# Attention and expert FFN on one core: routing sums earlier, transposes in twos, expert tiles turned elsewhere

## The chip, the cores and the metric

The kernel runs on one core of a Trainium2 chip. The metric is the device time of one execution in microseconds (us). Three timed runs of the kernel before gave 311.85, 312.05 and 313.8 us, with a median of 312.05 us. Engines are named as in the profile: PE (TensorE matmul), PEld (its weight loads), DVE (VectorE), ACT (ScalarE), POOL (GpSimd) and SP (SyncE, which here only issues transfers).

## The reference

Eight sequences of 576 tokens, with 8 heads of 64, go through attention that is causal by blocks of 64. Each token's 512 values then go through the one expert that a hash of its id names: two matmuls with a ReLU between them.

```python
scores = scale * np.matmul(q, k.transpose(0, 1, 3, 2))          # q, k, v: (8, 8, 576, 64)
scores = np.where(block_i >= block_j, scores, -1e9)             # blocks of 64 positions
attn = softmax(scores);  x = np.matmul(attn, v) -> (4608, 512)
expert_idx = token_ids * 2654435761 % 8
for e in range(8):                                              # w1: 512x1024, w2: 1024x512
    out[mask_e] = np.maximum(x[mask_e] @ w1[e], 0.0) @ w2[e]
```

## The kernel before

The order on every engine is that in which the code is written; nothing is scheduled afterwards. A tile's buffers are shared out by pools, and an instruction that needs a buffer waits until its last reader is done.

**Attention.** A sequence's 8 heads are worked on as 4 pairs, so the loop at L590 runs over 32 pairs g and two more rounds that only finish. Pair g belongs to sequence b = g // 4, and r = g % 4 is its place there. In a round PE computes the scores of pair g in three chunks (`S_chunk`, L222, written here S0, S1, S2), ACT takes the exponentials of each (L234, "exp"), and PE multiplies the probabilities of pair g - 2 with v in two halves (`PV`, L260). `norm` (L278) on DVE divides the result and thereby frees the PSUM tile `O`, of which there is one. So the first half of `PV` in a round waits for the `norm` of the round before. Score tiles `ps` have two buffers, so a chunk waits for the exp two chunks back. In the first round of a sequence `S_rest` adds one small chunk.

**Transposes of q and k.** The next sequence c needs q and k transposed. That is done in six groups of 12 transposes (`T_sixth`, L194; PE at L179), each followed by one copy out of PSUM (L186, on DVE; for sequence 1 every second one on ACT). The PSUM tile `tp` has two buffers. The list `at` (L580 to L584) says in which round and at which of five places each group stands: 0 ahead of S0, 1 behind S0, 2 behind S1, 3 behind S2, 4 behind `norm`.

**Routing.** `route` (L331) is a generator on DVE with a few matmuls. Each `next(rgen)` runs it to its next yield. For each sequence it makes one-hot tiles (`one_hots`, L322 to L326) and adds up slots by five matmuls (L430, into a `tp` buffer, added up at L433 or L435). `STEPS` and `TABLE` say in which rounds it goes on. The last steps (rounds 21 to 23) write the tables by which rows are gathered.

**From attention to FFN.** `write_x` (SP, L297) stores a sequence's result in `x_dram`. `load_x` (POOL, L306) gathers 128 rows of one expert. The first three tiles of each expert hold rows of sequences 0 to 5 alone, so they wait for the write of sequence 5; the last two wait for that of sequence 7. `turn_x` (L494) transposes one gathered tile (4 transposes, then one DVE copy, L499). `stage_a_early` (L501) computes two of the eight output blocks of expert 0's first matmul while attention ends. `stage_a` (L657) and `stage_b` (L675) are the two matmuls of the FFN; `stage_b` can take a list of tiles to turn, one behind each of its groups of eight matmuls.

Of the kernel before, what the change touches and what calls it, by code (L numbers as in the profile page):

```python
# [24 lines left out]
EB, ES = 6, 384  # L25
G = CAP // 128
# [12 lines left out]
def kernel(  # L39
# [248 lines left out]
    GE = ES // P  # L288
# [26 lines left out]
    def digits(out, tmp, src, shift, mask):  # L315
        nc.vector.tensor_single_scalar(tmp[:, 0, :, :], src[:], mask, op=ALU.bitwise_and)
        nc.vector.tensor_single_scalar(tmp[:, 1, :, :], src[:], shift, op=ALU.arith_shift_right)
        nc.vector.tensor_copy(out[:], tmp[:])
# [167 lines left out]
    NPAIRS = B * NP  # L486
# [69 lines left out]
    rgen = route()  # L556
# [14 lines left out]
    tok2 = rt.tile([P, 2, B, 5], I32, name="tok2", tag="i2")  # L571
    tokb = rt.tile([P, 2, B, 5], BF16, name="tokb")
    digits(tokb, tok2, toki, 6, 63)


    turned = {}
    for c in range(1, B):
        f = NP * c
        if c == 1:
            at = ((2, 4), (3, 1), (3, 2), (3, 3), (3, 4), (3, 4))  # L580
        elif c < 6:
            at = ((f - 3, 2), (f - 3, 3), (f - 2, 2), (f - 2, 3), (f - 1, 0), (f - 1, 3))
        else:
            at = ((f - 4, 3), (f - 3, 2), (f - 3, 3), (f - 2, 3), (f - 1, 0), (f - 1, 3))  # L584
        for n, gp in enumerate(at):
            turned.setdefault(gp, []).append((c, n))

    STEPS = {0: 3, 1: 2, 2: 1, 8: 1, 12: 1, 21: 1, 22: 1, 23: 1}
    TABLE = (8, 12, 16, 20)
    for g in range(NPAIRS + 2):  # L590
        b, r = divmod(g, NP)

        def turn(at):
            for c, n in turned.get((g, at), ()):
                T_sixth(c, n)
# [7 lines left out]
        if g < NPAIRS:  # L603
            S_chunk(g, 1)
        turn(2)
        if g == 3:
            next(rgen)
        if g < 2:
            fill(3)
        if g >= 2:  # L610
# [1 line left out]
        if g < NPAIRS:  # L612
            S_chunk(g, 2)
            if r == 0:
                S_rest(b)
        if g in TABLE or g == 3:
            next(rgen)
        turn(3)

        if g == NPAIRS - 1:  # L620
            for tt in range(GE):
                turn_x(0, tt, psT)
        if g >= NPAIRS:
            stage_a_early(0, g - NPAIRS)
        if g >= 2:
            PV(g - 2, 1)
            norm(g - 2)
        turn(4)
        for _ in range(STEPS.get(g, 0)):
            next(rgen, None)  # L630
        if r == 0 and b + 2 < B:
# [7 lines left out]
        if g == 23:  # L639
            after(load_w1(0), vparts[B - 1][1], "these bytes are wanted first")  # L640
            load_w1(1)
        if NPAIRS - 4 <= g < NPAIRS - 4 + GE:
            load_x(0, g - NPAIRS + 4, g - NPAIRS + 5)
        if g == NPAIRS:
            load_x(1, 0, GE)
            load_w2(0)
# [7 lines left out]
    psH = ffn_ctx.enter_context(tc.tile_pool(name="psH", bufs=2, space=PSUM))  # L654
    psX = ffn_ctx.enter_context(tc.tile_pool(name="psX", bufs=2, space=PSUM))
    psY = ffn_ctx.enter_context(tc.tile_pool(name="psY", bufs=2, space=PSUM))
    def stage_a(e, c0, c1, f0=0):  # L657
        w1b, _ = wtiles[e]
        xT, hT = xTs[e], hTs[e]
        parts = [(c0, c1)] if c1 - c0 <= 512 else [(c0, c0 + HC), (c0 + HC, c1)]  # L660
        n = parts[0][1] - parts[0][0]
        for ft in range(f0, NFT):
            hp = psH.tile([P, 2, 512], F32, name="hp", tag="hp")
            for db in range(NKT):
                for t, (p0, p1) in enumerate(parts):
                    nc.tensor.matmul(  # L666
                        hp[:, t, 0:n], lhsT=w1b[:, db, ft * P : (ft + 1) * P], rhs=xT[:, db, p0:p1],
                        start=(db == 0), stop=(db == NKT - 1),
                    )
            nc.scalar.activation(hT[:, ft, c0:c1].rearrange("p (t n) -> p t n", n=n),  # L670
                                 hp[:, 0 : len(parts), 0:n], ACT.Relu)

    out_writes = []

# [48 lines left out]
    for e in range(3):  # L723
        load_x(e, GE, G)
    load_w2(1)
    stage_a(0, 0, ES, 2)
    for tt in range(GE):
        turn_x(1, tt, psX)
    stage_a(1, 0, ES)
    stage_b(0, 0, GE)  # L730
    for tt in range(GE, G):
        turn_x(0, tt, psX)
    for e in range(E):
        if e + 2 < E:
            load_w1(e + 2)
# [204 lines left out]
```

## Time and profile before

| | |
|---|---|
| median of three timed runs | 312.05 us |
| the profiled execution | 310.51 us |
| its span, first to last instruction | 308.7 us |
| PE busy | 262.9 us (85%) |
| ACT busy | 149.6 us (48%) |
| DVE busy | 138.5 us (45%) |
| POOL busy | 133.1 us (43%) |

Attention runs from about 12 to 145 us of the span, with the switch to the FFN at about 134 to 145 us, and the FFN from there to about 300 us. The rows further down come from three views. The timeline has one line for a run of like instructions: its start in the span, how long it took, the engine, the source line, what is written from what, and in square brackets how long the engine had been idle and what released it. The table of windows gives each engine's busy time in a stretch. The view of a source line gives its instructions and how long its transfers took to land.

### The profile page before, as it was taken

To read this page: it belongs to the slowest core of one execution; us is meant where nothing else is said; L and a number is where in the kernel's file an instruction comes from. 1 tells how busy PE (TensorE), PEld (TensorE's weight loads), DVE (VectorE), ACT (ScalarE), POOL (GpSimd) and SP (SyncE) were. 2 spreads that over 40 slices of the span, in tenths; PEclk is the share of its full clock that TensorE was granted. 3 is DMA by queue.
4 is the path that set the end of the run, shared out by engine and by line. 5 is a ranking of instruction groups with operands and counts; after the bars stand their busy time and mean duration, and the time that the engine had idled before them with its cause. 6 is when DMAs were issued, how large, how long until landed. Compare 5 with 4: busy or idle time off the path is not lost. (4 is left out here: it accounts for less than half of the span.)

```text
span 308.7 us, 7626 instructions
## 1 busy us (share of the span) xinstructions
PE 262.9 (85%) x3224; PEld 172.6 (56%) x3241; DVE 138.5 (45%) x295; ACT 149.6 (48%) x193; POOL 133.1 (43%) x163
## 2 busy tenths in 40 slices
PE   7786788888878687768898999999999999999960
PEld 2455666666656565646545556556565564756620
DVE  6766477777676966342121251230513305034130
ACT  3694777777877787952523304215051240512400
POOL 8134231322222322283373662866748477323050
PEclk9997999999999999977999999999999999999996
DMA  6999999999998999559369999797998979812030
GB/s 107 208 196 197 211 189 218 197 197 221 179 205 166 207 199 215 112 179 188 109 110 222 209 234 272 169 190 241 181 275 178 220 226 192 268 60 107 2 139 14
DMA packets 65111, 55.63 MB, mean 180 GB/s; under 512 B 39973, under 2 KB 53797, under 8 KB 65072
## 3 DMA queue, kind: packets, MB, share of 16 engines
q0 software_dynamic: 22560, 40.90, 64.6%
q1 hardware_dynamic: 42512, 14.20, 19.9%
q8 instruction: 26, 0.43, 0.6%
q14 instruction: 13, 0.11, 0.1%
HBM read 67.15 MB, written 15.20 MB: 267 GB/s over the span
## 5 line engine op out<-in xcount | busy, mean ns | idle before, releaser
L234 ACT ACTIVATE pt<-ps 128x1024 bf16<-128x1024 f32 x96 | 92.3, 1027 | 25.0 <-PE ps L217 24.9
L670 ACT ACTIVATE hT<-hp 128x640 bf16<-128x640 f32 (+2 forms) x78 | 46.8, 600 | 98.9 <-PE hp L666 97.9
L666 PE MATMUL hp<-xT,w1b 128*128 128x320 bf16 (+2 forms) x504 | 72.3, 298 | 4.6 <-DVE xT L499 4.4
L682 PE MATMUL yp<-w2b,hT 128*128 128x512 bf16 x305 | 73.7, 379 | 0.8
L691 POOL DMA_INDIRECT out_dram<-ysb,perm x40 | 39.9, 997 | 56.9 <-DVE ysb L689 27.6
L666 PEld LDWEIGHTS <-w1b 128*128 128x128 bf16 x504 | 48.6, 97 | 25.8 <-issue 7.0
L499 DVE COPY xT<-tx 128x512 bf16<-128x512 bf16 x40 | 16.8, 424 | 92.6 <-PE tx L497 92.4
L306 POOL DMA_INDIRECT xg<-x_dram,tabi x40 | 41.1, 1027 | 30.9 <-issue 11.3
L272 PE MATMUL O<-vx,pt 128*128 128x65 bf16 x896 | 41.1, 198 | 12.2 <-DVE xs L283 12.0
L682 PEld LDWEIGHTS <-hT 128*128 128x128 bf16 x320 | 30.2, 98 | 30.3
L186 DVE COPY qkT<-tp 128x768 bf16<-128x768 bf16 x41 | 39.0, 953 | 16.6 <-PE tp L179 16.6
L272 PEld LDWEIGHTS <-pt 128*128 128x128 bf16 x896 | 33.4, 100 | 19.2 <-DVE xs L283 10.9
L208 PE MATMUL ps<-qkT 64*128 64x512 bf16 (+4 forms) x320 | 36.2, 296 | 8.5 <-DVE qkT L186 4.5
L689 DVE COPY ysb<-yp 128x512 f32<-128x512 f32 x40 | 27.3, 682 | 15.0 <-PE yp L682 15.0
L111 POOL DMA_DIRECT2D kb<-in_k_dram x9 | 6.7, 747 | 57.5 <-DMA vf<-in_v_dram 29.7
L208 PEld LDWEIGHTS <-qkT 64*128 64x128 bf16 x320 | 17.7, 94 | 21.1 <-DVE qkT L186 5.3
L283 DVE TENSOR_TENSOR xs<-O,rsall 128x640 bf16<-128x640 f32 x32 | 26.4, 824 | 1.1
L217 PE MATMUL ps<-maskq,maskk 64*128 64x64 bf16 x256 | 22.8, 190 | 0.0
L154 POOL CAST vx<-vf 128x2048 bf16<-128x2048 f32 x8 | 15.3, 1917 | 8.8 <-PE O L275 4.2
L497 PEld LDWEIGHTS <-xg 128*128 128x128 bf16 x160 | 12.2, 100 | 10.1 <-DMA xg<-x_dram,tabi 1.6
L497 PE MATMUL tx<-identbf,xg 128*128 128x128 bf16 x160 | 15.4, 224 | 1.8 <-DMA xg<-x_dram,tabi 1.4
L282 DVE RECIPROCAL rsall<-O 128x10 f32<-128x10 f32 x32 | 6.8, 213 | 18.2 <-PE O L275 18.2
(142 smaller groups left out, 180.0 us busy)
## 6 DMA issues: line engine op xcount, KB each, us to landing
vf<-in_v_dram SPq DMA_DIRECT2D x32, 256.0 KB, 8.1
w1b<-in_moe_w_dram POOLq DMA_DIRECT2D x8, 1024.0 KB, 8.5
w2b<-in_moe_w_dram POOLq DMA_DIRECT2D x8, 1024.0 KB, 13.4
x_dram<-xs SPq DMA_DIRECT2D x8, 512.0 KB, 8.5
kb<-in_k_dram POOLq DMA_DIRECT2D x7, 576.0 KB, 6.0
qb<-in_q_dram POOLq DMA_DIRECT2D x7, 576.0 KB, 9.6
vf<-in_v_dram SPq DMA_DIRECT2D x16, 64.0 KB, 4.5
xg<-x_dram,tabi POOLq DMA_INDIRECT x40, 9.6
```

Of the source, the lines that this page charges most:

```text
L186: ins = copy(qk[:, :, w, :].rearrange("p h (g j) -> p h g j", j=JR)[:, :, :, j0 + c0 : j0 + c1], tp[:, at[c0] : at[c1 - 1] + 1, :].rearran ...
L208: nc.tensor.matmul(ps[:, m, o0 : o0 + n], lhsT=qk[rows, r, 1, 128 * i : 128 * i + 128], rhs=qk[rows, r, 0, q0 : q0 + n], start=True, stop= ...
L234: nc.scalar.activation(ptv[:, :, 512 * ch : 512 * ch + 512], ps[:], ACT.Exp, scale=SCALE)
L272: nc.tensor.matmul(dst, lhsT=pt[:, o0 : o0 + 128], rhs=vx[:, h, i, :], start=(i == 0), stop=(i == t))
L283: nc.vector.tensor_tensor(out=xss[b % 2][:].rearrange("p t (m r d) -> p m t r d", m=2, r=NP)[:, :, :, r, :], in0=Ov[:, :, :, 0:D], in1=rs[ ...
L306: r = nc.gpsimd.indirect_dma_start(out=xgs[e][:, gg, :], out_offset=None, in_=x_dram[0:rows, :], in_offset=bass.IndirectOffsetOnAxis(ap=ta ...
L497: nc.tensor.transpose(out=tp[:, db, :], in_=xgs[e][:, tt, db * P : (db + 1) * P], identity=identbf[:])
L666: nc.tensor.matmul(hp[:, t, 0:n], lhsT=w1b[:, db, ft * P : (ft + 1) * P], rhs=xT[:, db, p0:p1], start=(db == 0), stop=(db == NKT - 1),)
L670: nc.scalar.activation(hT[:, ft, c0:c1].rearrange("p (t n) -> p t n", n=n), hp[:, 0 : len(parts), 0:n], ACT.Relu)
L682: nc.tensor.matmul(yp[:], lhsT=hT[:, ft, tt * P : (tt + 1) * P], rhs=w2b[:, ft, :], start=(ft == 0), stop=(ft == NFT - 1),)
L689: nc.vector.tensor_copy(ysb[:], yp[:])
L691: ins = nc.gpsimd.indirect_dma_start(out=out[:, :], out_offset=bass.IndirectOffsetOnAxis(ap=perm3[:, gg : gg + 1], axis=0), in_=ysb[:], in ...
```

## The change

Five things are moved; no instruction is added or removed.

1. The first two one-hots are made at the end of round 1 instead of round 2. Their sums stand behind S2 in rounds 2 and 3, instead of at two places of round 3.
2. For sequences 2 to 7 the six groups of transposes stand two by two behind S1, in each of the three rounds ahead of the sequence.
3. Expert 0's first three tiles are turned at the end of round 31, behind the second half of `PV` and `norm`, and no longer ahead of that half. Both `stage_a_early` blocks stand at the end of round 32, instead of one each inside rounds 32 and 33.
4. The three `load_x` for these tiles are issued one round earlier.
5. `stage_a` also takes a list of tiles to turn. Expert 1's first three tiles are turned one by one behind the first three groups of `stage_a(0, ...)`, and expert 0's last two behind groups of `stage_b(0, ...)`; before, both lots stood in a row between stages.

```diff
+    TABLE = (8, 12, 16, 20)
@@
-        elif c < 6:
-            at = ((f - 3, 2), (f - 3, 3), (f - 2, 2), (f - 2, 3), (f - 1, 0), (f - 1, 3))
         else:
-            at = ((f - 4, 3), (f - 3, 2), (f - 3, 3), (f - 2, 3), (f - 1, 0), (f - 1, 3))
+            at = [(g, 2) for g in range(f - 3, f) for _ in range(2)]
@@
-    STEPS = {0: 3, 1: 2, 2: 1, 8: 1, 12: 1, 21: 1, 22: 1, 23: 1}
-    TABLE = (8, 12, 16, 20)
+    STEPS = {0: 3, 1: 3, 8: 1, 12: 1, 21: 1, 22: 1, 23: 1}
@@
         turn(2)
-        if g == 3:
-            next(rgen)
@@
-        if g in TABLE or g == 3:
+        if g in TABLE or g in (2, 3):
             next(rgen)
         turn(3)
-
-        if g == NPAIRS - 1:
-            for tt in range(GE):
-                turn_x(0, tt, psT)
-        if g >= NPAIRS:
-            stage_a_early(0, g - NPAIRS)
         if g >= 2:
             PV(g - 2, 1)
             norm(g - 2)
         turn(4)
+
+        if g == NPAIRS - 1:
+            for tt in range(GE):
+                turn_x(0, tt, psT)
+        if g == NPAIRS:
+            for ft in range(2):
+                stage_a_early(0, ft)
@@
-        if NPAIRS - 4 <= g < NPAIRS - 4 + GE:
-            load_x(0, g - NPAIRS + 4, g - NPAIRS + 5)
+        if NPAIRS - 5 <= g < NPAIRS - 5 + GE:
+            load_x(0, g - NPAIRS + 5, g - NPAIRS + 6)
@@
-    def stage_a(e, c0, c1, f0=0):
+    def stage_a(e, c0, c1, f0=0, turns=()):
@@
+            if turns:
+                turn_x(*turns.pop(0), psX)
@@
-    stage_a(0, 0, ES, 2)
-    for tt in range(GE):
-        turn_x(1, tt, psX)
+    stage_a(0, 0, ES, 2, [(1, tt) for tt in range(GE)])
     stage_a(1, 0, ES)
-    stage_b(0, 0, GE)
-    for tt in range(GE, G):
-        turn_x(0, tt, psX)
+    stage_b(0, 0, GE, [(0, tt) for tt in range(GE, G)])
```

On DVE, rounds 1 to 3, before the change (L316 to L318 end round 1, L282 and L283 are the `norm` of pair 0 in round 2, L322 to L326 the one-hots, L433 and L435 the sums, L186 the copies of transposes):

```order
L318 CAST dig<-lo_i 128x80
L282 RECIPROCAL rsall<-O 128x10
L283 TENSOR_TENSOR xs_127<-O,rsall 128x2x5x64
L322 TENSOR_TENSOR hots<-dig,iota_c 128x640
L324 TENSOR_TENSOR ones_hi<-dig,iota_c 128x200
L326 TENSOR_TENSOR hots<-ones_hi,tokb 128x400
L322 TENSOR_TENSOR hots<-dig,iota_c 128x640
L324 TENSOR_TENSOR ones_hi<-dig,iota_c 128x200
L326 TENSOR_TENSOR hots<-ones_hi,tokb 128x400
L186 COPY qkT<-tp 128x4x32x6
L433 COPY acc<-pt__576 128x80
L435 TENSOR_TENSOR acc<-pt__609,acc 128x80
```

The same place with the change:

```order
L318 CAST dig<-lo_i 128x80
L322 TENSOR_TENSOR hots<-dig,iota_c 128x640
L324 TENSOR_TENSOR ones_hi<-dig,iota_c 128x200
L326 TENSOR_TENSOR hots<-ones_hi,tokb 128x400
L322 TENSOR_TENSOR hots<-dig,iota_c 128x640
L324 TENSOR_TENSOR ones_hi<-dig,iota_c 128x200
L326 TENSOR_TENSOR hots<-ones_hi,tokb 128x400
L433 COPY acc<-pt__499 128x80
L282 RECIPROCAL rsall<-O 128x10
L283 TENSOR_TENSOR xs_127<-O,rsall 128x2x5x64
L186 COPY qkT<-tp 128x4x32x6
L435 TENSOR_TENSOR acc<-pt__609,acc 128x80
```

The six one-hot instructions and the first sum now stand ahead of the `norm` of pair 0, and no longer between that `norm` and the first DVE copy of sequence 1's transposes.

On DVE, from the last rounds of attention into the FFN, before the change (L499 copies a turned expert tile, L689 copies a finished group of `stage_b`; L282 and L283 are the `norm` of a round):

```order
L499 COPY xT<-tx 128x4x128 x3
L282 RECIPROCAL rsall<-O 128x10
L283 TENSOR_TENSOR xs_128<-O,rsall 128x2x5x64
L282 RECIPROCAL rsall<-O 128x10
L283 TENSOR_TENSOR xs_128<-O,rsall 128x2x5x64
L282 RECIPROCAL rsall<-O 128x10
L283 TENSOR_TENSOR xs_128<-O,rsall 128x2x5x64
L499 COPY xT<-tx 128x4x128 x3
L689 COPY ysb<-yp 128x512 x3
L499 COPY xT<-tx 128x4x128 x3
L689 COPY ysb<-yp 128x512
```

The same place with the change:

```order
L282 RECIPROCAL rsall<-O 128x10
L283 TENSOR_TENSOR xs_128<-O,rsall 128x2x5x64
L499 COPY xT<-tx 128x4x128 x3
L282 RECIPROCAL rsall<-O 128x10
L283 TENSOR_TENSOR xs_128<-O,rsall 128x2x5x64
L282 RECIPROCAL rsall<-O 128x10
L283 TENSOR_TENSOR xs_128<-O,rsall 128x2x5x64
L499 COPY xT<-tx 128x4x128 x4
L689 COPY ysb<-yp 128x512
L499 COPY xT<-tx 128x4x128
L689 COPY ysb<-yp 128x512 x2
```

The copies of expert 0's first three tiles have moved behind the `norm` of pair 29, and those of expert 0's last two tiles now stand between the output copies of `stage_b(0)`.

## Rows read from the trace of the kernel before

**Rows 1.** Windows: length, then busy us (instructions) of PE, PEld, DVE, ACT, POOL, clock, DMA share, GB/s.
```profile
80.60:91.51 10.91, 9.42 (x219) 7.10 (x217) 8.54 (x13) 8.70 (x9) 4.07 (x5) 1.00 0.97 169
95.97:107.81 11.84, 8.96 (x206) 6.72 (x205) 10.81 (x26) 8.89 (x9) 4.26 (x5) 1.00 1.01 192
133.98:144.73 10.75, 6.99 (x99) 5.55 (x96) 3.36 (x7) 2.12 (x4) 6.45 (x7) 0.68 0.77 145
180.00:200.00 20.00, 19.52 (x129) 11.72 (x130) 6.04 (x12) 5.63 (x8) 10.70 (x11) 1.00 0.97 220
```

**Rows 2.** Timeline of round 19: start, us, engine, line, tiles, forms, count, [idle before <-releaser].
```profile
87.90 0.39 PE L208 MATMUL ps<-qkT 64*128 64x512 bf16 x2
88.09 0.82 DVE L283 TENSOR_TENSOR xs<-O,rsall 128x640 bf16<-128x640 f32 x1
...
88.42 2.85 ACT L234 ACTIVATE pt<-ps 128x1024 bf16<-128x1024 f32 x3 [0.82 <-PE ps L217]
...
88.97 0.62 PE L272 MATMUL O<-vx,pt 128*128 128x65 bf16 x14 [0.40 <-DVE xs L283]
...
89.55 0.31 PE L208 MATMUL ps<-qkT 64*128 64x320 bf16 x2
...
89.93 0.53 PE L179 MATMUL tp<-identbf,qb 128*64 128x128 bf16 x12
90.39 0.62 PE L272 MATMUL O<-vx,pt 128*128 128x65 bf16 x14
90.50 0.96 DVE L186 COPY qkT<-tp 128x768 bf16<-128x768 bf16 x1 [0.72 <-PE tp L179]
...
91.51 0.39 PE L208 MATMUL ps<-qkT 64*128 64x512 bf16 x2 [0.48 <-DVE qkT L186]
```

**Rows 3.** Timeline of rounds 1 to 4: the one-hots, their first sum, and the next sequence.
```profile
21.20 0.22 DVE L282 RECIPROCAL rsall<-O 128x10 f32<-128x10 f32 x1 [2.21 <-PE O L275]
...
22.20 0.55 DVE L322 TENSOR_TENSOR hots<-dig,iota_c 128x640 bf16<-128x640 bf16 x1
...
24.06 0.41 DVE L326 TENSOR_TENSOR hots<-ones_hi,tokb 128x400 bf16<-128x400 bf16 x1
...
25.19 0.72 PE L430 MATMUL pt__576<-hots 128*128 128x80 bf16 x5 [1.96 <-ACT qkT L186]
...
31.71 0.39 PE L208 MATMUL ps<-qkT 64*128 64x512 bf16 x2 [1.25 <-DVE qkT L186]
```

**Rows 4.** Source line L297, the two writes of sequence 5's result.
```profile
L297 SPq DMA_DIRECT2D x_dram<-xs x2: 392/454/517, 116.6 to 117.1; - x2
...
DMA to landing us min/median/max: 11.3/11.4/11.6
```

**Rows 5.** Source line L306, the first three gathers.
```profile
L306 POOL DMA_INDIRECT xg<-x_dram,tabi x3: 1006/1036/1098, 129.3 to 132.0; - x3
...
DMA to landing us min/median/max: 3.2/4.1/5.1
```

**Rows 6.** Timeline of PE from attention into the FFN.
```profile
135.80 1.04 PE L497 MATMUL tx<-identbf,xg 128*128 128x128 bf16 x8 [1.42 <-DMA xg<-x_dram,tabi]
...
138.84 0.95 PE L272 MATMUL O<-vx,pt 128*128 128x65 bf16 x14 [1.18 <-DVE xs L283]
...
143.12 0.62 PE L272 MATMUL O<-vx,pt 128*128 128x65 bf16 x14 [1.17 <-DVE xs L283]
```

**Rows 7.** Timeline of PE in the FFN, behind tiles that are turned in a row.
```profile
149.83 0.38 PE L497 MATMUL tx<-identbf,xg 128*128 128x128 bf16 x4 [0.36 <-DVE xT L499]
...
150.82 1.46 PE L666 MATMUL hp<-xT,w1b 128*128 128x384 bf16 x8 [0.61 <-DVE xT L499]
...
163.07 4.25 PE L666 MATMUL hp<-xT,w1b 128*128 128x256 bf16 x32 [1.00 <-DVE xT L499]
```

**Rows 8.** Timeline of PE in round 3, a group of transposes while the clock was low.
```profile
27.89 0.85 PE L179 MATMUL tp<-identbf,qb 128*64 128x128 bf16 x12
```

**Rows 9.** Window around it, columns as in the first group.
```profile
26.00:30.00 4.00, 4.00 (x69) 3.08 (x68) 1.61 (x5) 1.02 (x1) 2.52 (x3) 0.57 1.01 162
```

More of the change, by code (lines that the diff above doesn't have):

```diff
@@ L661, in stage_a @@
         n = parts[0][1] - parts[0][0]
+        turns = list(turns)
         for ft in range(f0, NFT):
```

## The prediction

> **What bounds the kernel now.** I read the windows first. In the FFN PE is busy 19.52 of 20 us and its clock is full, so there only PE work or a PE wait counts [rows 1]. In attention nothing is full: in rounds 17 to 19 (80.60 to 91.51) PE is busy 9.42 of 10.91 us, ACT 8.70 and DVE 8.54. The loop loses time to waits between them. In rounds 21 to 23 it is DVE that is nearly full, 10.81 of 11.84 us. Between attention and FFN (133.98 to 144.73) PE is busy 6.99 of 10.75 us at a mean clock of 0.68.
>
> Then the timeline names the waits. In round 19 the first half of `PV` waits 0.40 us for `norm` (DVE xs), and the next sequence's S0 waits 0.48 us for the last copy of a group [rows 2]. In round 3 the first sum waits 1.96 us, and S0 of round 4 waits 1.25 [rows 3]. At the switch PE waits 1.42 us for a gathered tile and 1.18 and 1.17 for `norm` [rows 6], and in the FFN 0.36, 0.61 and 1.00 us for copies of tiles turned in a row [rows 7].
>
> **Transposes in twos.** From start to start, round 19 gives the PE cost of each piece [rows 2]: S0 and S1 0.67 (88.97 less the wait of 0.40, less 87.90), half a `PV` 0.58 (88.97 to 89.55), S2 0.38 (to 89.93), a group 0.46 (to 90.39). The new round is S0, S1, group, group, `PV`, S2, `PV`: 0.67 + 0.92 + 0.58 + 0.38 + 0.58 = 3.13 us. The `norm` of the round before ends 1.01 us after S0 starts (88.09 + 0.82). PE now reaches `PV` at 1.59, so the wait of 0.40 is gone. DVE takes the two copies behind that `norm`, 0.96 each, from about 1.2 to 3.1, and is free as this round's `PV` ends. The next sequence's S0 then waits for next to nothing, where it waited 0.48.
>
> ACT sets a second limit. Three exps take 2.85 [rows 2]. S2 now starts at 2.17, later by two groups; an exp starts about 0.5 behind its chunk (87.90 to 88.42), so the third ends near 3.6. The next S1 needs its buffer at 3.13 + 0.3, so it waits about 0.2. I take 3.33 us for a round, 10.0 for three, against 10.91 now: 0.9 less. Four sequences (2 to 5) have this form and I take them alike: 3.6. Sequence 7 also frees its first round from a group, half hidden behind ACT: 0.9 + 0.3 = 1.2. For sequence 6 I take nothing: in its three rounds DVE is already busy 10.81 of 11.84 us with five of the groups and the table steps [rows 1]. The sixth copy adds 0.96, 11.8 in all, so DVE fills the stretch however PE is ordered. Sum 4.8 us. The bounds are 3 (half the gain in sequences 2 to 5) and 7 (no wait for ACT: 0.2 in each of the 12 rounds before sequences 2 to 5, 2.4 us, comes back).
>
> **One-hots and sums.** The six one-hot instructions (22.20 to 24.47) move into a stretch in which DVE stands idle for 2.21 us ahead of 21.20 [rows 3]. They fit but for some 0.2 us, by which the first `norm` is later; the rounds behind hide that. In round 2 PE has the sum 0.7 us longer, and that much less in round 3. The wait of 1.96 was for a `tp` buffer that ACT copies out behind exps. With the sum gone from there, the group behind S2 meets that wait. `PV`, S2 and the second sum (0.58 + 0.38 + 0.7) now come first and hide most of it; about 0.5 is left. The 1.25 in front of round 4 is the copy behind round 3's `norm`, which stays late by about half. So 1.5 + 0.7 = 2.2 us; bounds 1 and 3.2 (both waits whole).
>
> **The switch to the FFN.** Attention gives 7.0 us so far (bounds 4 and 10). What stands in the way is the gathered tile. The write of sequence 5 is issued at 116.6 and lands 11.3 to 11.6 later, at 128.2 or so [rows 4]; only then does the first gather start, at 129.3 [rows 5]. Issuing `load_x` a round earlier on POOL therefore gives nothing: POOL has stood waiting, and its queue holds nothing that would go out sooner. The last of the three gathers is issued at 132.0 and lands by 136.1, taking its median of 4.1.
>
> Does that write land earlier if attention is 7 us ahead? It can't gain more than 7. It gains nothing if transfers are what paces it, and in rounds 17 to 19 the DMA share is 0.97 [rows 1]. I take the middle, 3.5: there is more than one transfer ahead of it, but rounds that end sooner also issue sooner. The last tile then lands at 132.6 and is turned by 133.0. PE is there at 133.98 - 7.0 + 0.6 (the moved half of `PV`) = 127.6, and waits up to 4 us for the three tiles, since they come one behind the other. Behind the tiles come two rounds of `PV` and the two early blocks. Now they take 5.89 us from 138.84 to 144.73, of which 1.17 is a wait for `norm` [rows 6]; the tiles and the early blocks now stand where both `norm` waits were, so 4.7 are left, at the clock that this stretch has now. `stage_a` starts at 137.7, 7.0 ahead of 144.73. If the write doesn't move, it starts at 136.1 + 0.4 + 4.7 = 141.2, 3.5 ahead. If it moves by all 7, at 134.2, 10.5 ahead.
>
> **The FFN.** The same transposes and copies stand singly between groups, where the trace shows such tiles in `stage_b` without a wait. The three waits go: 0.36 + 0.61 + 1.00 = 1.97, say 2.0 us [rows 7]; less than 1 if the gathered tiles are late, nothing below nothing, as no work is added.
>
> **Sum.** 7.0 + 2.0 = 9.0 us off. The profiled execution took 310.51 us, so it would take 301.5. The median of the timed runs is 1.54 above that execution; off 312.05 the forecast is **303.0 us**.
>
> **Rivals.**
>
> *The write of sequence 5 doesn't move.* For it: the DMA share of 0.97, and 11.3 us from issue to landing. Against it: writes that are issued sooner stand further ahead in the queue. It gives 3.5 + 2.0 = 5.5 off, 306.5 us. The same time comes out if the loop gains nothing at all, since its gain only passes through this point. It decides for itself whenever the landing stays near 128.
>
> *All of it arrives.* The write moves in full, or rounds 17 to 19 are as short as 3.13: 10.5 + 2.0 = 12.5 off, 299.5 us. For it: PE has 1.49 us idle in each such stretch [rows 1]. Against it: DMA again.
>
> *The clock falls in the rounds with two groups (slower than before).* In a window of the old trace that follows the 1.96 us wait the mean clock is 0.57, that is mostly at 1.2 GHz [rows 9], and a group takes 0.85 there against 0.53 [rows 8, 2]. A round at that rate would take 3.13 x 0.85 / 0.53 = 5.0 us, 1.7 more than forecast. With 18 such rounds the gain of 9.0 is gone when 6 of them run low, and if all did the time would be 303.0 + 30 = 333 us. Against it: in rounds 17 to 19 the clock is 1.00 with the same six groups and with more idle time than I expect [rows 1]. The Trainium skill speaks for it: "TensorE: Matmul & The Clock Gate", section "Part 4: PE-mode transpose", says that the full clock doesn't engage for transposes, because they do not count as PE work in the same way. By that rule two groups side by side look like a longer rest, and the time would be this rival's. In single groups the trace does not bear it out; two in a row with full rounds around them it doesn't show.
>
> *It does nothing that can be measured.* The waits could turn up elsewhere: ACT is busy 8.70 of 10.91 us and DVE 8.54. For that the switch too would have to give nothing, and its 3.5 come from the order on PE alone. 310 to 312 us.
>
> **How the numbers follow.** Forecast 0.50, write unmoved 0.22, all of it 0.15, clock falls 0.06, nothing 0.07. The range reaches from all of it, with 2 us for the bound of 7 in the loop, to the unmoved write, with 2 us for FFN waits that stay: 297.5 to 308.5. What is left out is the last two and the far ends of the rest. About 1% (3.1 us) is what a measurement of this kernel can tell from no change. Faster by over 1%: 0.50 + 0.22 + 0.15 = 0.87; within it 0.07; slower 0.06.
>
> **What would show it.** Rounds 17 to 19 last about 10.0 us, with no wait of `PV` for `norm`, and S1 waits some 0.2 us for an exp. Rounds 21 to 23 don't get shorter and DVE fills them. The wait of a sum in round 3 is gone, and round 4 starts near 29.5. PE waits for the gathered tile at about 128 to 132, and the clock falls there as now. `stage_a` follows without a wait for `norm`, and no transposed tile is waited for in the FFN. The forecast is wrong if the write of sequence 5 lands at the same time, if the granted clock falls in rounds 5 to 27, or if copies run into the next round's `norm`.

## The result, and the profile after

The changed kernel took 304.16 us (median of four runs, 301.05 to 305.02). The kernel before, timed beside it, took 312.93 (311.85 to 315.01). The ratio is 0.969, with a 95% interval of 0.961 to 0.978. The forecast was 303.0 in a range of 297.5 to 308.5, with faster at 0.87.

The profiled execution took 304.37 us (span 302.5) where the one of before took 310.51, so there the gain is 6.1 us and not the 9.0 of the sum. The medians differ by 8.8, since the profiled execution of before was quicker than its timed runs (311.85 at least). The points below are settled between the two traces.

Windows of the changed kernel: rounds 17 to 19, rounds 21 to 23, the switch (columns as in [rows 1]):

```profile
77.34:87.12 9.78, 9.25 (x221) 7.20 (x220) 8.61 (x13) 8.22 (x9) 3.96 (x5) 1.00 1.07 195
91.11:103.63 12.52, 9.22 (x218) 7.16 (x217) 12.06 (x26) 8.71 (x9) 4.14 (x5) 1.00 1.01 207
127.00:137.35 10.35, 7.83 (x128) 6.00 (x125) 4.28 (x9) 4.39 (x6) 8.22 (x9) 0.84 0.42 110
```

Rounds 17 to 19 went from 10.91 to 9.78 us. Rounds 21 to 23 went from 11.84 to 12.52, with DVE busy 12.06 of it.

Timeline of the changed kernel, a round with two groups and the one behind it:

```profile
77.94 0.86 PE L179 MATMUL tp<-identbf,kb 128*64 128x128 bf16 x24
78.51 1.82 DVE L186 COPY qkT<-tp 128x768 bf16<-128x768 bf16 x2
78.73 0.62 PE L272 MATMUL O<-vx,pt 128*128 128x65 bf16 x14
...
80.28 0.39 PE L208 MATMUL ps<-qkT 64*128 64x512 bf16 x2
...
80.94 0.37 PE L208 MATMUL ps<-qkT 64*128 64x448 bf16 x2 [0.24 <-ACT pt L234]
```

The 24 transposes take 0.86 us, `PV` behind them has no wait, where it had 0.40 in [rows 2], and the next S1 waits 0.24 for an exp.

Where the gain went, read from the first exp of a round and from the first block of `stage_a`:

| stretch | before | after | difference | forecast |
|---|---|---|---|---|
| rounds 0 to 3 | 19.31 | 17.37 | -1.94 | -2.2 |
| rounds 4 to 7 | 14.52 | 14.55 | +0.03 | -0.9 |
| rounds 8 to 11, 12 to 15, 16 to 19 | 15.18, 15.18, 14.92 | 14.21, 14.21, 13.75 | -0.97, -0.97, -1.17 | -0.9 each |
| rounds 20 to 23 | 16.30 | 16.54 | +0.24 | 0 |
| rounds 24 to 27 | 14.99 | 13.95 | -1.04 | -1.2 |
| `stage_a` starts at | 144.73 | 137.35 | -7.38 | -7.0 |
| from there to `stage_a` of the late tiles | 18.34 | 19.65 | +1.31 | -2.0 |

So the loop and the switch came out near the forecast, and the FFN lost where it should have gained. PE in that stretch of the changed kernel, which answers to [rows 7]:

```profile
137.35 0.81 PE L664 MATMUL hp<-xT,w1b 128*128 128x384 bf16 x4
...
147.57 1.89 PE L682 MATMUL yp<-w2b,hT 128*128 128x512 bf16 x8
151.41 0.40 PE L497 MATMUL tx<-identbf,xg 128*128 128x128 bf16 x4 [1.96 <-DMA xg<-x_dram,tabi]
151.65 2.64 PE L682 MATMUL yp<-w2b,hT 128*128 128x512 bf16 x8
154.09 0.63 PE L497 MATMUL tx<-identbf,xg 128*128 128x128 bf16 x4
...
157.00 4.25 PE L664 MATMUL hp<-xT,w1b 128*128 128x256 bf16 x32
```

The three old waits are gone. In their place PE waits 1.96 us for tile (0,3), the fourth of expert 0, and the group behind it takes 2.64 us instead of 1.89. Windows of the stretches in which the granted clock was low, and of 40 us of attention:

```profile
33.17:36.58 3.41, 3.41 (x53) 2.55 (x51) 1.52 (x3) 2.61 (x4) 0.12 (x1) 0.50 1.16 235
60.00:100.00 40.00, 36.67 (x815) 28.34 (x811) 33.16 (x61) 34.14 (x38) 11.00 (x13) 1.00 1.05 212
104.85:108.26 3.41, 3.39 (x51) 2.36 (x49) 1.01 (x5) 2.60 (x5) 0.00 (x0) 0.50 1.14 260
132.16:135.57 3.41, 2.98 (x37) 2.50 (x38) 1.08 (x3) 0.00 (x0) 2.92 (x3) 0.50 0.32 91
152.64:156.05 3.41, 3.41 (x13) 1.46 (x11) 1.30 (x3) 0.00 (x0) 2.80 (x3) 0.50 0.39 112
```

Each low stretch comes behind waits of PE: 1.32 us ahead of 30.38, 2.82 ahead of 103.63, 2.1 in three pieces from 129.7 to 132.6, and 1.96 ahead of 151.41. Such a wait doesn't always bring one: in a later run of the same kernel PE waits 1.33 us ahead of round 4 too, and the clock stays at 1.00 from 24 to 40 us. A granted clock of 0.50 is 1.2 GHz, so where PE has work throughout, half of the 3.41 us is lost, by estimate some 1.7 us on top of the wait. Where two-group rounds follow one another (60 to 100 us) the clock is 1.00.

Tile (0,3) is late because the write of sequence 7 is. Source line L297 of the changed kernel, the two writes of sequence 5 and then those of sequence 7:

```profile
L297 SPq DMA_DIRECT2D x_dram<-xs x2: 393/466/539, 112.0 to 112.4; - x2
...
DMA to landing us min/median/max: 12.7/13.2/13.7
```
```profile
L297 SPq DMA_DIRECT2D x_dram<-xs x2: 380/520/661, 138.7 to 139.1; - x2
...
DMA to landing us min/median/max: 9.0/9.0/9.0
```

The same line before the change, for sequence 7:

```profile
L297 SPq DMA_DIRECT2D x_dram<-xs x2: 381/856/1332, 146.0 to 146.5; - x2
...
DMA to landing us min/median/max: 3.4/3.4/3.4
```

Before, the load of w2(0), the second matrix of expert 0 (1 MB), went out on POOL's queue at 137.0 and was in at 145.9, just ahead of that write. Now it goes out at 134.65 and the write four microseconds behind it. The DMA queues of the changed kernel (packets, MB, share) show what the write meets. The first two lines are all queues from 138.7, its issue, to 143.0; the last is its own queue from 143.0 to 147.7:

```profile
q0 software_dynamic: 619, 0.64, 106.1%
q8 instruction: 1, 0.02, 1.4%
...
q1 hardware_dynamic: 608, 0.59, 35.8%
```

So for 4.3 us not one packet of the write moves, while POOL's queue (q0) moves 619. The gathers for tiles (0,3) and (0,4) start only at 148.6.

### The profile page after: what moved, and what is told of

Its sections match the earlier page's. It is cut to its first block, busy times and chain, and to the rows that moved or that the text cites. A ratio compares the mean times of both kernels' runs of the same rounds, so it can differ in the third digit from the quotient of the medians.

```text
span 302.5 us, 7644 instructions
## 1 busy us (share of the span) xinstructions
PE 266.0 (88%) x3241; PEld 173.9 (57%) x3241; DVE 141.1 (47%) x295; ACT 149.6 (49%) x193; POOL 132.9 (44%) x163
## 5 line engine op out<-in xcount | busy, mean ns | idle before, releaser
L682 PE MATMUL yp<-w2b,hT 128*128 128x512 bf16 x320 | 76.5, 385 | 0.0
L499 DVE COPY xT<-tx 128x512 bf16<-128x512 bf16 x40 | 17.0, 424 | 100.6 <-PE tx L497 100.6
L306 POOL DMA_INDIRECT xg<-x_dram,tabi x40 | 41.1, 1027 | 34.8 <-DMA x_dram<-xs 18.7
L208 PE MATMUL ps<-qkT 64*128 64x512 bf16 (+4 forms) x320 | 39.2, 302 | 12.6 <-ACT pt L234 6.1
L186 DVE COPY qkT<-tp 128x768 bf16<-128x768 bf16 x41 | 37.5, 952 | 8.2 <-PE tp L179 8.2
L208 PEld LDWEIGHTS <-qkT 64*128 64x128 bf16 x320 | 19.1, 95 | 27.1 <-issue 10.6
L689 DVE COPY ysb<-yp 128x512 f32<-128x512 f32 x40 | 27.3, 682 | 6.8 <-PE yp L682 6.8
L283 DVE TENSOR_TENSOR xs<-O,rsall 128x640 bf16<-128x640 f32 x32 | 26.4, 824 | 1.1
L282 DVE RECIPROCAL rsall<-O 128x10 f32<-128x10 f32 x32 | 7.0, 219 | 19.4 <-PE O L275 16.8
```

What stands on the lines that cost most here:

```text
L186: ins = copy(qk[:, :, w, :].rearrange("p h (g j) -> p h g j", j=JR)[:, :, :, j0 + c0 : j0 + c1], tp[:, at[c0] : at[c1 - 1] + 1, :].rearran ...
L208: nc.tensor.matmul(ps[:, m, o0 : o0 + n], lhsT=qk[rows, r, 1, 128 * i : 128 * i + 128], rhs=qk[rows, r, 0, q0 : q0 + n], start=True, stop= ...
L283: nc.vector.tensor_tensor(out=xss[b % 2][:].rearrange("p t (m r d) -> p m t r d", m=2, r=NP)[:, :, :, r, :], in0=Ov[:, :, :, 0:D], in1=rs[ ...
L306: r = nc.gpsimd.indirect_dma_start(out=xgs[e][:, gg, :], out_offset=None, in_=x_dram[0:rows, :], in_offset=bass.IndirectOffsetOnAxis(ap=ta ...
L682: nc.tensor.matmul(yp[:], lhsT=hT[:, ft, tt * P : (tt + 1) * P], rhs=w2b[:, ft, :], start=(ft == 0), stop=(ft == NFT - 1),)
L689: nc.vector.tensor_copy(ysb[:], yp[:])
```

## The experiments

The twelve kernels ran in three groups of four, and in all of them the kernel before takes longer than above: its medians there are 319.13 us (the four that undo a part), 322.35 (the next four) and 321.3 (the last four). Each ratio is to the kernel before in the same group. The changed kernel itself ran only in the last group, so the totals of the first eight can't be held against it. Where a total was expected of them, the measured one lies above it, and none shows what its part is worth in the total. What is read is waits, the landing of writes, and stretches of the traces. Rounds 8 to 19 repeat within 0.2 us in every kernel that has the groups in twos. Rounds 0 to 7 and 20 to 23 differ by microseconds between traces of one program, so there the waits count and not the length.

**The groups of transposes back in their old places.**

```diff
-            at = [(g, 2) for g in range(f - 3, f) for _ in range(2)]
+            at = ((f - 3, 2), (f - 3, 3), (f - 2, 2), (f - 2, 3), (f - 1, 0), (f - 1, 3))
+            if c >= 6:
+                at = ((f - 4, 3), (f - 3, 2), (f - 3, 3), (f - 2, 3), (f - 1, 0), (f - 1, 3))
```

> The changed kernel with the transposes of sequences 2 to 7 back in their six old places; everything else as changed. Theory: the loop loses what its rounds 4 to 27 gained between the two traces (96.4 to 92.4... 91.1 us from the first exp of round 4 to that of round 28 before, 87.2 after, so 3.9), and PE reaches the gathered tiles that much later; about 2.5 to 4 us slower than the changed kernel, 306.5 to 308. Rival: the write of sequence 5 is paced by transfers, so the loop's gain never reaches the FFN: within 1 us of the changed kernel.

311.95 us, ratio 0.976 (0.969 to 0.983). Timeline of PE, rounds 17 to 19:

```profile
81.00 0.39 PE L208 MATMUL ps<-qkT 64*128 64x512 bf16 x2
...
85.86 0.60 PE L272 MATMUL O<-vx,pt 128*128 128x65 bf16 x14 [0.49 <-DVE xs L283]
...
89.37 0.62 PE L272 MATMUL O<-vx,pt 128*128 128x65 bf16 x14 [0.41 <-DVE xs L283]
91.91 0.39 PE L208 MATMUL ps<-qkT 64*128 64x512 bf16 x2 [0.48 <-DVE qkT L186]
```

From 81.00 to 91.91 is 10.91 us again, to the hundredth, with the same waits for `norm` and for the copy. Rounds 8 to 19 lose 3.1 us against the changed kernel's trace, where the loop term had 2.7.

**The one-hots and sums back.** The six one-hots go to round 2 and both sums to round 3:

```diff
-    STEPS = {0: 3, 1: 3, 8: 1, 12: 1, 21: 1, 22: 1, 23: 1}
+    STEPS = {0: 3, 1: 2, 2: 1, 8: 1, 12: 1, 21: 1, 22: 1, 23: 1}
@@
+        if g == 3:
+            next(rgen)
@@
-        if g in TABLE or g in (2, 3):
+        if g in TABLE or g == 3:
```

> The changed kernel with the one-hots back at the end of round 2 and both sums in round 3. Theory: from the first exp to round 4 it takes 19.3 us again and not 17.4, and 1 to 2 us of that reach the end: 305 to 306. Rival: the loads of q, k and v pace the loop, and the early gain is waited away later: within 0.5 us of the changed kernel.

308.93 us, ratio 0.967 (0.960 to 0.974). Rounds 0 to 3 take 19.33 us, against 17.32 in the kernel with the groups back. That alone shows little: with the one-hots where the change puts them, the kernel with the FFN's tiles in a row and the one with w2(0) moved (both further down) take 21.04 and 19.64, each with 6.8 us of low clock from 22 to 30 us. In the timeline of PE the first sum waits again, as in [rows 3]:

```profile
25.63 0.72 PE L430 MATMUL pt__576<-hots 128*128 128x80 bf16 x5 [1.96 <-ACT qkT L186]
```

None of the kernels with the one-hots moved has this wait; in five of those traces the first sum, a round earlier, waits 0.5 to 0.7 us for a one-hot instead. So the part removes 1.96 us of waiting in round 3. In the total it can't be told from noise.

**The tiles and early blocks back in their old places** (tiles ahead of the last half `PV` of round 31, one early block each in rounds 32 and 33).

```diff
+        if g == NPAIRS - 1:
+            for tt in range(GE):
+                turn_x(0, tt, psT)
+        if g >= NPAIRS:
+            stage_a_early(0, g - NPAIRS)
         if g >= 2:
             PV(g - 2, 1)
```

> The changed kernel with expert 0's first tiles turned ahead of the last PV half of round 31 again, and the early blocks inside rounds 32 and 33; the gathers stay one round earlier. Theory: the two waits of 1.2 us for norm come back and half a PV stands behind the tiles; 3 to 3.5 us slower than the changed kernel, about 307.5. Rival: the landing of the gathered tiles sets the time there whatever stands around it: within 1 us.

311.33 us, ratio 0.974 (0.967 to 0.981). In the timeline of PE both waits for `norm` are back at the size that they had [rows 6]; what they cost can't be read off here, since a stall that is told of below lies in the same stretch:

```profile
139.90 0.95 PE L272 MATMUL O<-vx,pt 128*128 128x65 bf16 x14 [1.17 <-DVE xs L283]
...
144.19 0.95 PE L272 MATMUL O<-vx,pt 128*128 128x65 bf16 x14 [1.17 <-DVE xs L283]
```

**The FFN's tiles turned in a row again.**

```diff
-    stage_a(0, 0, ES, 2, [(1, tt) for tt in range(GE)])
+    stage_a(0, 0, ES, 2)
+    for tt in range(GE):
+        turn_x(1, tt, psX)
     stage_a(1, 0, ES)
-    stage_b(0, 0, GE, [(0, tt) for tt in range(GE, G)])
+    stage_b(0, 0, GE)
+    for tt in range(GE, G):
+        turn_x(0, tt, psX)
```

> The changed kernel with expert 1's first and expert 0's last tiles turned in a row between the stages again. Theory by the trace of the changed kernel: its 1.96 us wait for expert 0's fourth tile and the low clock behind it eat what the three old waits (1.97 us) gave, so this is within 1 us of the changed kernel, either way. Rival, the prediction's term: 2.0 us slower, 306.2.

310.11 us, ratio 0.967 (0.958 to 0.976). Timeline of PE in the FFN, with the waits of [rows 7]:

```profile
146.15 4.29 PE L664 MATMUL hp<-xT,w1b 128*128 128x384 bf16 x24
151.25 0.38 PE L497 MATMUL tx<-identbf,xg 128*128 128x128 bf16 x4 [0.36 <-DVE xT L499]
152.24 5.62 PE L664 MATMUL hp<-xT,w1b 128*128 128x384 bf16 x32 [0.61 <-DVE xT L499]
...
164.49 1.68 PE L664 MATMUL hp<-xT,w1b 128*128 128x256 bf16 x12 [1.00 <-DVE xT L499]
```

The stretch is 18.34 us long (146.15 to 164.49), as before the change. In the kernels with the groups back and with the one-hots back, which keep the new FFN, it is 15.84. So the edit in the FFN by itself gives 2.5 us where the write is not in the way, and the expectation, no difference, failed. In those two kernels the write of sequence 7 is issued 9.6 us and more behind the load of w2(0), and lands within 3.3.

**The table's steps later.** The indices for the gathers are made in round 21, the rest in rounds 28 to 30.

```diff
+        nc.vector.scalar_tensor_tensor(out=tabf[:, 0:NM], in0=acc[:, NM:], scalar=64.0, in1=acc[:, 0:NM],
+                                       op0=ALU.mult, op1=ALU.add)
+        nc.vector.tensor_copy(tabi[:, 0:NM], tabf[:, 0:NM])
+        yield
         eo = rt.tile([1, OVT, E], F32, name="eo")
@@
-    STEPS = {0: 3, 1: 3, 8: 1, 12: 1, 21: 1, 22: 1, 23: 1}
+    STEPS = {0: 3, 1: 3, 8: 1, 12: 1, 21: 1, 28: 1, 29: 1, 30: 1}
```

> The changed kernel with the routing's last steps taken out of rounds 21 to 23: the gather table (tabi) is made in round 21, and the steps that only the FFN's stores and the general path need come in rounds 28 to 30, where no transposes are copied. Theory: DVE is what fills sequence 6's rounds, so the wait of S0 of round 24 (2.82 us) shrinks to below 0.5, rounds 20 to 23 take about 14 us and not 16.5, and 1.5 to 2.5 us reach the end: 301.5 to 302.5. Rival: the landing of sequence 5's write does not follow, so PE only waits longer for the gathered tiles: within 0.7 us of the changed kernel.

310.07 us, ratio 0.960 (0.953 to 0.967). Rounds 20 to 23 take 14.47 us instead of 16.54, and round 24 starts without a wait. So what DVE does beside the copies kept sequence 6 from gaining; the next run shows that much of it was no work. The 2 us are lost again in round 30, as the timeline of DVE shows:

```profile
122.15 0.22 DVE L282 RECIPROCAL rsall<-O 128x10 f32<-128x10 f32 x1 [0.47 <-PE O L275]
127.53 0.82 DVE L283 TENSOR_TENSOR xs<-O,rsall 128x640 bf16<-128x640 f32 x1 [5.15 <-DMA x_dram<-xs]
```

There are two `xs` buffers, so `norm` of sequence 7 writes where the write of sequence 5 still reads. That write was issued at 112.3 and landed 15.0 us later, at 127.3, and PE stood still for 5.09 us. In the changed kernel's first trace this write landed at 126.07 and that `norm` started at 127.2: the next wall was 1.1 us away.

**The cast of v one round later,** out of DVE's full round.

```diff
-        if r == 2 and b + 1 < B:
+        if r == 3 and b + 1 < B:
             cast_v(b + 1)
```

> The changed kernel with POOL's cast of v one round later in each sequence (r = 3 and not 2). Only one look, for one instruction: in the changed kernel DVE's L450 took 1.53 us beside POOL's cast of v and ended with it; before it took 0.17 us where no cast ran. Theory: a DVE instruction of this kind can stand still as long as POOL casts, so L450 takes about 0.17 us here. Rival: it waits for its operands, and takes 1.5 us here too.

314.0 us in its one run, against 322.35. The point is on DVE. First the timeline of the changed kernel in round 23, POOL, DVE, and PE's next sequence; then that of this kernel:

```profile
98.57 1.89 POOL L154 CAST vx<-vf 128x2048 bf16<-128x2048 f32 x1 [0.87 <-PE ps L208]
98.96 1.53 DVE L450 TENSOR_TENSOR pvalid<-base,jg 128x24 f32<-128x24 f32 x1
...
103.63 0.39 PE L208 MATMUL ps<-qkT 64*128 64x512 bf16 x2 [2.82 <-DVE qkT L186]
```
```profile
100.47 1.89 POOL L154 CAST vx<-vf 128x2048 bf16<-128x2048 f32 x1 [0.85 <-PE tp L179]
...
102.31 0.86 POOL L157 CAST v<-vf 64x256 bf16<-64x256 f32 x2
102.89 0.31 DVE L450 TENSOR_TENSOR pvalid<-base,jg 128x24 f32<-128x24 f32 x1
...
106.06 0.39 PE L208 MATMUL ps<-qkT 64*128 64x512 bf16 x2 [1.33 <-DVE qkT L186]
```

L450 takes 1.53 us when it starts under the cast, and ends as the cast does (100.49 and 100.46). Behind the large cast it takes 0.31, and the wait of PE falls from 2.82 to 1.33. Not the 0.17 expected, because here it starts under a small cast (L157), with which it ends (103.20 and 103.17).

**The load of w1(1) (expert 1's first matrix, 1 MB) three rounds later,** in round 26, and then **the gathers for expert 1 and the load of w2(0) in rounds 30 and 31.**

```diff
-            load_w1(1)
+        if g == 26:
+            load_w1(1)
```

> The changed kernel with the load of expert 1's w1 (1 MB) issued in round 26 and not in round 23. Theory: the write of sequence 5 lands late because it shares the DMA engines with two weight loads; with one it lands within 8 us of its issue and not 12.7 to 13.7, PE's waits for the first three gathered tiles (0.46, 0.66 and 0.96 us) go, and 1.5 to 2.5 us reach the end: about 302. Rival: the write is held up by the loads of v ahead of it in the same queue: it lands as late as now and nothing changes.

```diff
-        if g == NPAIRS:
-            load_x(1, 0, GE)
-            load_w2(0)
-            load_x(2, 0, GE)
+        if g == 30:
+            load_x(1, 0, GE)
+        if g == 31:
+            load_w2(0)
+        if g == NPAIRS:
+            load_x(2, 0, GE)
```

> The changed kernel with expert 1's first three gathers in round 30 and the load of expert 0's w2 (1 MB) in round 31, so that this load starts a few us sooner than the write of sequence 7. Theory: the two share the DMA engines now, and that is why the write takes 9.0 us; apart it takes 3 to 5, the wait of 1.96 us for expert 0's fourth tile and the low clock behind it go, 2 to 3 us less: 301 to 302. Rival: the gathers and the load are issued from POOL in order behind the gathers that wait for sequence 5, so the load starts no sooner, and the time is that of the changed kernel.

With w1(1) later: 311.02 us, ratio 0.970 (0.962 to 0.977). The write of sequence 5 lands 8.8 to 9.1 us after its issue, and the first gather starts at 121.8 instead of 127.0. That the load moved is the reason is not shown: in the kernel with the tiles and early blocks back, whose loads stand as in the changed kernel, it lands after 8.9 and 9.3. Rounds 29 and 30 then take 5.4 and 8.8 us, and the gain is gone. With the gathers and w2(0) moved: 311.55 us, ratio 0.967 (0.962 to 0.972). Here nothing moved, since POOL's queue stands at the first gather until the write of sequence 5 has landed: w2(0) went out at 136.4.

In this trace and in six others of the first eight (that with w1(1) later among them), a stall turned up that neither of the first two traces has. By the profile, which models the ends of matmuls, PE is done with a chunk of scores and a half `PV`, and ACT and DVE, which wait for them, go on only 3 to 6 us later. So the changed kernel itself was run beside the last three.

> The changed kernel itself, measured beside the next three on one chip. On the chips of the runs that undo one part, the kernel before took 319 to 322 us where it took 312.9 beside the first run of the changed kernel, and seven of eight variants show a stall of PE of 4 to 6 us while the nine gathers are being issued, which neither of the first two traces has: PE has finished (a block's sums end at 131.93), and VectorE, which waits for them, goes on only at 138.26. Theory A, the stall belongs to the chip and not to the variants: on a chip where the kernel before takes 319 us or more this kernel shows it too, loses 4 to 6 us at the switch, takes 307 to 311 us, and its write of sequence 7 is then issued 9 us or more after the load of w2(0) and lands within 3.5 us, without a wait at tile (0,3). Theory B, the variants cause it: no stall here, 301 to 305 us. On a chip where the kernel before takes 313 us the first traces repeat: 304 us, a wait of about 2 us at tile (0,3), ratio 0.969.

307.08 us (305.71 to 309.15), ratio 0.964 (0.957 to 0.971). Timeline of this run at the switch:

```profile
131.17 0.20 PE L275 MATMUL O<-v,pt 128*128 128x65 bf16 x1
131.20 0.33 PE L497 MATMUL tx<-identbf,xg 128*128 128x128 bf16 x3
...
134.83 1.02 ACT L234 ACTIVATE pt<-ps 128x1024 bf16<-128x1024 f32 x1 [3.88 <-remote]
134.92 0.22 DVE L282 RECIPROCAL rsall<-O 128x10 f32<-128x10 f32 x1 [5.61 <-remote]
...
136.38 0.59 PE L497 MATMUL tx<-identbf,xg 128*128 128x128 bf16 x4 [3.52 <-DVE xT L499]
```

`PV` ends at 131.4 and the reciprocal that waits for it starts at 134.92. So the stall comes with these runs and not with the variants, as far as one trace can tell. What holds ACT and DVE the profile doesn't name. In each of the ten runs that have it, it begins in the stretch in which POOL issues the nine gathers. The write of sequence 7 is then issued 10 us behind w2(0) and lands in 2.9, there is no wait at tile (0,3), and the FFN's stretch is 15.84 us (142.45 to 158.29 in the timeline of PE):

```profile
142.45 0.81 PE L664 MATMUL hp<-xT,w1b 128*128 128x384 bf16 x4
...
158.29 4.24 PE L664 MATMUL hp<-xT,w1b 128*128 128x256 bf16 x32
```

**Tiles (0,3) and (0,4) one group later.**

```diff
-    stage_b(0, 0, GE, [(0, tt) for tt in range(GE, G)])
+    stage_b(0, 0, GE, [None] + [(0, tt) for tt in range(GE, G)])
```

> The changed kernel with the two tiles (0,3) and (0,4) transposed one output group later (behind the second and third group of expert 0 instead of the first and second). The theory that the FFN's term was lost to the write of sequence 7: tile (0,3) lands at 151.37 in the first trace, the second group would end at 151.3, so the wait of 1.96 us at it falls under 0.3 us and the low clock of 152.6 to 156.1 behind it, which cost about 1.7 us more, is gone: 3 to 3.6 us faster than the changed kernel where that one shows the wait, nothing (within 0.5 us) where the stall at the switch has let the write land first. Rival, the wait only moves to tile (0,4) or to the second stage behind it: no gain in either case.

308.43 us (307.10 to 309.35), ratio 0.967 (0.961 to 0.973): nothing gained, and nothing to gain, since the changed kernel beside it had no wait there. The rival came true in part: the wait moves to the second stage, where tile (0,4) is now turned straight ahead of it (timeline of PE).

```profile
158.42 1.79 PE L664 MATMUL hp<-xT,w1b 128*128 128x256 bf16 x13 [1.12 <-issue]
```

The stretch from `stage_a` is 17.58 us against 15.84 beside it, and 16.5 in the next two kernels, which have this edit too. Whether it pays where the wait for tile (0,3) exists stays open. The trace shows something else. Up to the FFN the program is that of the changed kernel, but here the cast came late by itself (POOL waited for PE), and L450 ran free (timeline of DVE, POOL and PE, then the window of rounds 21 to 23):

```profile
98.14 0.17 DVE L450 TENSOR_TENSOR pvalid<-base,jg 128x24 f32<-128x24 f32 x1
...
100.86 1.89 POOL L154 CAST vx<-vf 128x2048 bf16<-128x2048 f32 x1 [1.57 <-PE O L275]
101.18 0.39 PE L208 MATMUL ps<-qkT 64*128 64x512 bf16 x2 [1.20 <-DVE qkT L186]
```
```profile
90.28:101.18 10.90, 9.22 (x219) 7.17 (x217) 10.43 (x26) 8.70 (x9) 1.75 (x3) 1.00 0.98 207
```

Rounds 21 to 23 take 10.90 us here, where the changed kernel's first trace has 12.52 and the kernel before 11.84. The same instruction took 1.15 under the cast in the run of the changed kernel beside it, and the wait at round 24 was 2.60. What this run gained there it lost in round 30, where `norm` waited 3.70 us for the write of sequence 5 (13.9 to 14.2 us to land).

**Both load moves with that.** The three diffs above together.

> As the last one, with the load of w1(1) issued three rounds later (round 26, behind the write of sequence 5, which is issued in round 25) and the gathers for expert 1 and the load of w2(0) issued in rounds 30 and 31 ahead of the attention's last pass. If the two 1 MB loads in front of it are what makes the write of sequence 5 take 12.7 us to land, it lands within 9.5 us, as in the run with w1(1) alone moved (9.1 against 12.7), and the first gather is issued 3 to 5 us earlier (about 123 where the changed kernel has 127.0); w2(0) is then issued near 130 and is through before the write of sequence 7. The waits of 0.46, 0.66 and 0.96 us at the first three tiles and half of the low clock behind them go: 2 to 4 us faster than the changed kernel. Rival, the load of w1(1) then lies on the gathers and on the loop's last rounds, as rounds 29 and 30 of that run with 5.4 and 8.8 us: no gain, or slower by 1 to 4 us.

308.31 us (305.57 to 311.84), ratio 0.964 (0.956 to 0.972): no gain over the 307.08 of the changed kernel beside it. The write of sequence 5 still took 12.4 to 13.0 us, with w1(1) issued 3.5 us behind it. It was 8.2 us behind in the run with w1(1) alone (9.1 at most), and 6.5 in the next one (11.0). The three would fit a load that starts while the write is under way and slows it. That isn't shown: with both loads in front or beside it the write took from 8.9 us (the tiles back in their old places) to 15.0, and what sets its time stays open.

**And the table's steps later too.** All four diffs together.

> As the last one, with the table's remaining vector work taken out of rounds 22 and 23 (the indices that the gathers want are made in round 21, the rest in rounds 28 to 30). The run with this part alone showed rounds 20 to 23 at 14.47 us against 16.53, without the wait of 2.82 us at round 24 and without the low clock behind it, and lost it again at round 30, where the norm of sequence 7 waited for the write of sequence 5 (issued 112.3, landed 127.3) to free its buffer. If that write was all that took it back, then with the write landing by 122 the loop ends 3.5 to 4 us earlier than in the changed kernel and the time is 4 to 7 us below the changed kernel's. Rival, VectorE's steps in rounds 28 to 30 or the switch itself take it back: within 1.5 us of the kernel with the loads moved.

304.10 us (302.79 to 305.66), ratio 0.954 (0.948 to 0.960). All six runs are below all six of the changed kernel beside it, and the medians differ by 3.0 us, less than the 4 to 7 expected. Rounds 20 to 23 take 13.75, the write of sequence 5 lands by 121.7, no `norm` waits for it, and the first gather starts at 122.6. The stall is still there (DVE stands 5.97 us), so what this order gives without it is not known.

## Why the prediction was right, and where a term was off

The time fell inside the range, 1.2 us above the point, and by the mechanism that carried the most weight up to the FFN. That it came so near is in part luck: between the two traces the gain is 6.1 us and not 9.0, and the rest comes from timed runs of the kernel before that lay 1.3 to 4.5 us above its profiled execution. By its own steps:

- **Transposes in twos: right.** A round was put at 3.33 us, and the rounds of a sequence last 2.93, 3.35 and 3.47, mean 3.25. The wait for `norm` went, S1 waits 0.24 where 0.2 was forecast, and undoing the part brings back 10.91 us.
- **Sequences 2 to 5 alike: wrong for one.** Rounds 4 to 7 gained nothing. The old low-clock stretch lay in rounds 2 and 3 [rows 9]. It is now at 33.17 to 36.58, behind the 1.32 us wait that stayed, and costs about what the order gave. In the later run of the changed kernel, whose clock stays at 1.00 from 24 to 40 us, these rounds take 13.22, so there the order gives 1.3.
- **Sequence 6 nothing: the number right, the reason only in part.** DVE is busy 12.06 of 12.52 us, but 1.4 of that is L450 standing still under POOL's cast. Where it ran free, rounds 21 to 23 took 10.90, 0.9 less than before, with DVE busy 10.43. So the order gave here what it gave elsewhere, and the cast took it back. The 11.8 us that were to fill the stretch took standing for work: before, an instruction of the table (L439) took 1.23 us beside the cast, against 0.40 beside none. That DVE's work is the limit behind this holds: with the table's steps gone, rounds 20 to 23 fall to 14.47 and 13.75, from 14.90 where L450 ran free.
- **One-hots and sums: the size right, 1.94 for 2.2, one of its two terms not.** The 1.96 us wait is gone. The wait ahead of round 4 stayed whole, 1.32 for 1.25 [rows 3], where 0.7 of it was to go. And part of the 1.94 is the low-clock stretch that left these rounds: over rounds 0 to 7 the gain is 1.9 us of the 3.1 forecast, and 3.9 in the later run without that stretch.
- **The switch: right, 7.38 for 7.0.** The write of sequence 5 was issued 4.6 us earlier and landed 2.3 to 3.6 earlier; half of 7 had been assumed. PE turned the tiles from 130.2 to 132.6, and the last had landed at 132.5, with 132.6 forecast. From there to `stage_a` it took 4.8 us, with 5.1 forecast. Since the landing of this write sets the place where PE waits, the 1.2 us that the loop gave less shows little here.
- **The FFN: the mis-sized term,** +1.3 us instead of -2.0. The sum took the three waits out and said "nothing below nothing, as no work is added". The edit does give 2.5 us (18.34 to 15.84 where it is undisturbed). The step that failed is that the late tiles' transfers were left where they had been. The write of sequence 7, issued 7 us earlier with everything around it, met the load of w2(0), whose own issue had moved by only 2.3. It took 9.0 us instead of 3.4, and PE paid 1.96 of wait and, by estimate, about 1.7 of low clock. The gap between 9.0 and 6.1 us in the profiled executions is this term (3.3), less 0.4 that the switch gave more.
- **The clock in two-group rounds: that rival did not come.** The clock is 1.00 from 60 to 100 us, and 24 transposes take 0.86 us. A sign that the prediction set for being wrong did show all the same: the granted clock fell in rounds 4 and 5 and in 24 and 25, but behind the waits of 1.32 and 2.82 us, not in the rounds where pair follows pair. The Trainium skill, "TensorE: Matmul & The Clock Gate", section "Part 4: PE-mode transpose", says that the full clock does not engage for transposes. Two groups with matmuls on both sides do not bear that out here.

Why the kernel before takes 6 to 9 us more in the experiments' groups than beside the first run, and the changed kernel only 3, stays open: the kernel before has no trace there.

## What to carry to other kernels

When one stage is made shorter, list the transfers whose issue moves with it, and look up which other transfer each will now meet. Here a write that landed in 3 us at a quiet place took 9 behind a 1 MB load, and that cost more than the FFN's removed waits gave (by estimate 3.7 us against 2.5). A reordering that removes small waits can also move a stretch of low clock behind the ones that stay, as it did here, so its gain is best read over several rounds and more than one trace. An engine that a view calls busy can be standing: compare one instruction's time with the same instruction elsewhere before a stretch is called full. And a gain early in the program counts only up to the next point that waits for a transfer.

## What the hardware showed that was not expected

**DVE under a cast on POOL.** L450, on 24 columns, took 0.17 us in the seven traces in which no cast ran beside it, and 0.9 to 1.9 in the five in which it started with 0.8 us or more of the large cast still to run (1.53 in the timeline above, 1.15 in the later run of the changed kernel). It ended within 0.05 us of the cast each time. The copies out of PSUM do not show it: beside the cast L186 takes 0.95 as elsewhere. The Trainium skill, "SBUF — State Buffer", section "SBUF: two separate sides", says that POOL and a DVE instruction with two SBUF inputs share a pair of ports as an exclusive lock, and that the loser is blocked for the whole instruction. L450 has two SBUF inputs, and the trace agrees.

**Writes beside loads.** The write of sequence 7 landed after 2.9 to 3.4 us when w2(0) was issued 9 us or more ahead of it, after 3.8 when 8.9 ahead, after 5.5 and 5.9 when 7.5 and 6.8 ahead, and after 9.0 when 4 ahead. Put otherwise, in the seven traces in which w2(0) was issued 4 to 9.6 us ahead, the write landed 12.5 to 13.0 us behind the issue of that load. So its landing went by the load's issue and not by its own. The Trainium skill, "DMA: Bandwidth & Descriptors", section "Queues, rings and completion order", says that each engine takes turns between its queues packet by packet. For the first 4.3 us of the write in the changed kernel the trace does not agree: its queue has no packet there, and POOL's has 619. Whether the write's packets were passed over or not yet in the queue, no run here shows.

**A stall at the switch.** In ten of the twelve runs PE stands still for about 3 to 6 us while POOL issues gathers, and in neither of the first two traces. The two without it are those in which `norm` in round 30 waits for the write of sequence 5 ahead of the first gather. What it is stays open.
